# A gated recurrence with a fused two-layer product on one core: the engine queues from a listed order, more transposes by DMA, and casts shared between two engines

## The chip, the cores and the metric

The kernel runs on one core of a Trainium2 chip. The core has a matrix engine (PE, with its weight loads shown as PEld), a vector engine (DVE), a scalar engine (ACT), GpSimd (POOL), and a sync engine (SP) which here issues nearly all DMAs. Each engine works through its own instruction queue in program order, and waits in it on semaphores of other engines. The metric is the device time of one launch in microseconds (us), lower is better; a time is the median over several runs.

## What is computed

```python
for t in range(S):                                # S = 768, for 4 batches x 8 heads, D = 48
    state = alpha[t][:, None] * state + outer(k[t], v[t])
    y[t] = q[t] @ state
x = y.transpose(0, 2, 1, 3).reshape(3072, 384)    # tokens x (heads * D)
h = x @ w_in                                      # 384 -> 2048
g = relu(h) ** 2
out = g @ w_out                                   # 2048 -> 384, fp32
```

All inputs and the output are fp32. The kernel works in bf16 with fp32 sums.

## The kernel before

**Tiling.** The 3072 tokens are 24 chunks of 128, six for each batch. The recurrence is done chunk by chunk, all 8 heads at once; the state between chunks is kept in a PSUM bank (`st`). Chunks 0 to 3 are done as two sets of two with other code (`add_set`); chunks 4 to 23 with `add_chunk`. Two chunks share one scores step from chunk 8 on.

**One chunk** (`s`), in the words that the text below uses; the lines are those of the profile:

- Four loads of 192 KB (at, q, k, v; L388, in six buffers each), issued by SP.
- ln of alpha on ACT (L447), `p0`: its running sum on PE, exp of it and of its negative on ACT (`Af` L728, `Ainv` L735), v to bf16 on POOL (`vb` L716), and two tiny DMAs on POOL's queue for the row that decays the state (`ae` L746).
- q times `Af` and k times `Ainv` on DVE into `qk_s` (`mq` L777, `mk` L782).
- The transposes of both into `qkT`. For chunks 4 to 15: eight PE transposes (`p1q`, `p1k`, L298) and a DVE copy out of PSUM (`cp`, L714). For chunks 16 to 23: one transposing DMA on SP's queue, called a turn here (L799).
- `p2`: the scores on PE, then the causal mask. For chunks 4 to 7 both halves are DVE multiplies (L833); from chunk 8 the second half is an ACT copy (L836) and a select on POOL (L839).
- `ps`, the state's update: PE, DVE multiply (L867), ACT copy `sb` (L873). `p3a` and `p3b`: y on PE.
- y to bf16 (`xn`, L712, ACT), three PE transposes (`p4`, L298) and a copy of x transposed into `xT_big` (L714; DVE or ACT).

**The two products.** The tokens are taken in 12 groups: g0 holds chunks 0 to 3, g1 chunk 4, g2 chunk 5, g3 to g11 two chunks each. The first product (`add_moe1`, "M1") multiplies `w_in` with `xT_big` in blocks of 128 of the 2048 columns (f0 to f15); ACT does the relu (L990), DVE squares it into `gT` (L1009). The second product of g0 to g2 ("M2") is plain; from g3 on (`add_moe2_pair`) two chunks go together with seven block products P1 to P7 in place of eight, which need sums on DVE (S1 to S4, L1172 and L1182), four sums of `w_out` blocks done once (`foldT`, L1106), and small copies out of PSUM (ca, cu, cy, L1212/L1214, on ACT or DVE; c12, L1231/L1233; c11, c21 and c22, L1229, on DVE).

**The weights.** `w_in` comes in five pieces and `w_out` in four (L363), through four staging buffers; each piece is cast to bf16 by POOL (L366). The first two pieces of `w_in` hold two blocks each, the others four.

**What sets the order.** The kernel builds a list of operations (`Op`), each with an engine (or two to choose from), a planned duration, dependencies and buffers. `Plan.run` simulates the engines with these numbers and picks at each step, for the engine that comes free first, the operation that can start first (ties by a priority). It adds a slack of 0.25 to 0.3 us to waits of PE on other engines. The operations are then sorted by planned start and emitted, so that each engine's queue has this order. Loads keep the order in which they were added. Where the plan sees PE idle before the first M2, the program fills the idle time with dummy matmuls on a `warm` tile.

Of the kernel before, what the change touches and what calls it, by code (L numbers as in the profile page):

```python
# [64 lines left out]
class Plan:  # L65


    def __init__(self):
        self.pending = {}
        self.order = []  # L70
        self.free = {}
        self.pool = []
        self.outs = []
        self.wide = []

    def add(self, op):
        op.durs = op.eng if isinstance(op.eng, dict) else {op.eng: op.dur}
        for e in op.durs:
            self.pending.setdefault(e, []).append(op)
        return op  # L80
# [30 lines left out]
    def run(self, gate):  # L111
        free = self.free
        while any(self.pending.values()):
            best = None
            for eng, ops in self.pending.items():
                t0 = free.get(eng, 0.0)
                pick = None
                fifo = eng in ("DMA",)
                for op in (ops[:1] if fifo else ops):
                    if not gate(op):  # L120
                        continue
                    r = self.ready(op)
                    if r is None:
                        continue
                    if len(op.durs) > 1:
                        ends = {e: max(r, free.get(e, 0.0)) + x + LAT[e] for e, x in op.durs.items()}
                        if ends[eng] > min(ends.values()):
                            continue
                    key = (max(r, t0), op.prio)
                    if pick is None or key < pick[0]:  # L130
                        pick = (key, op)
                if pick is not None and (best is None or pick[0][0] < best[0]):
                    best = (pick[0][0], eng, pick[1])
            assert best is not None, "nothing can run"
            t, eng, op = best
            for e in op.durs:
                self.pending[e].remove(op)
            op.eng, op.dur = eng, op.durs[eng]
            while eng == "DMA" and self.outs and min(self.outs)[0] <= t:
                out = min(self.outs)  # L140
                self.outs.remove(out)
                t += out[1]
            op.start = t + getattr(op, "late", 0.0)
            if eng == "POOL":
                if not op.quiet:
                    self.pool.append((t, t + op.dur))
            elif eng == "DVE" and op.shared:
                for a, z in self.pool[-3:]:
                    op.dur += POOL_SHARE * max(0.0, min(z, t + op.dur) - max(a, t))
            free[eng] = t + op.dur  # L150
            if op.lat is None:
                op.lat = LAT.get(eng, 0.2)
            if eng == "OUT":
                self.outs.append((op.start, op.moves or op.dur))
            elif op.moves:
                self.outs.append((op.start + op.dur, op.moves))
            op.done = t + op.dur + op.lat
            if op.takes is not None:
                self.ready(op)
                for i, sl in enumerate(op.slots):  # L160
                    gives = op.gives if op.gives is not None else op
                    sl.release.append(gives[i] if op.n_slots > 1 else gives)
            self.order.append(op)
            self.on_pick(op)
        self.order.sort(key=lambda o: o.start)


@with_exitstack
def kernel(
# [33 lines left out]
    LB = 6  # L203
# [68 lines left out]
    CP_FLEX = 0  # L272
# [34 lines left out]
    SEL_FROM, SEL_T, SEL_N = 8, 0.6, 1  # L307
# [3 lines left out]
    VB_ACT = 99  # L311
# [4 lines left out]
    plan.slack = 0.3  # L316
    QT_FROM, QT_DMA, QT_LAT = 16, 1.8, 2.7
    XT_FROM, XT_DMA, XT_LAT = 99, 0.7, 2.3
# [16 lines left out]
    LD1 = 1.1  # L335
    LD2 = 1.5
    WLD = {"i": 2.05, "o": 2.4}
# [8 lines left out]
    SB = 4  # L346

    def load_w(which):
        j = len(w_ready[which])
        lo, hi = W_CUT[which][j:j + 2]  # L350
        n = hi - lo
        box = {}

        if which == "i":
            src, dst = w_in_r[:, :, lo * P:hi * P], w_in_b[:, :, lo * P:hi * P]
            shape = [P, KT, n * P]
        else:
            src, dst = w_out_r[:, lo:hi, :], w_out_b[:, lo:hi, :]
            shape = [P, n, d_model]

        def e_issue():
            box["w"] = stage.tile(shape, FP32, name=f"w{which}{n}", tag="stage")
            pin(nc.sync.dma_start(out=box["w"], in_=src))  # L363

        def e_cast():
            pin(nc.gpsimd.tensor_copy(dst, box["w"]))  # L366
        prev = w_cast[-SB] if len(w_cast) >= SB else None
        ld = add("DMA", WLD[which] * (0.85 if n < 4 else n / 4.0), e_issue, prev, lat=2.2)
        op = add("POOL", 0.1 + 0.32 * n, e_cast, ld, prio=-3.0)
        w_cast.append(op)  # L370
        w_ready[which].append(op)

    def w_dep(which, f):
        return w_ready[which][[hi > f for hi in W_CUT[which][1:]].index(True)]

    C = [dict() for _ in range(NT)]
    state = {}
# [3 lines left out]
    def add_load(s, nm):  # L381
# [8 lines left out]
        d["ld_" + nm] = add("DMA", LD if s < 4 else LD1, ld, prev, lat=L_ADD + (2.6 if s < 6 else 3.2 if s < 8 else 4.0), at=0.6)  # L390

    def add_decay2(s):
# [11 lines left out]
        ld = add("DMA", LD2, ld, C[s - LB]["use_at"] if s >= LB else None, lat=L_ADD + (2.6 if s < 6 else 3.2 if s < 8 else 4.0), at=0.6)  # L404
# [65 lines left out]
    def add_load2(u, nm, a=None):  # L470
# [8 lines left out]
        op = add("DMA", LD2 * (hi - lo) / H, ld, lat=2.5, at=0.6)  # L479
# [3 lines left out]
    def add_set(u):  # L483
# [163 lines left out]
        def add_out(c):  # L647
# [45 lines left out]
            p4.gives = xT  # L693
        for c in range(2):
            add_state(c)
            add_out(c)
        C[s0]["end"] = C[s0 + 1]["end"]
        for e in C[s0:s0 + 2]:
            e["use_at"], e["use_qt"], e["use_kt"], e["use_vt"] = ln[1], mq[1], mk[1], vb

    def add_chunk(s):
# [20 lines left out]
        vb = d["use_vt"] = add({"ACT": 0.37} if s >= VB_ACT else {"POOL": 0.5}, 0, e_vb, d["ld_vt"], *old, prio=-5.0)  # L722
# [60 lines left out]
        mq = d["use_qt"] = add("DVE", 0.767 if AMODE == "str" else 0.47, e_qA, a_, d["ld_qt"], *old_of(s, "p1q"), **g)  # L783
# [16 lines left out]
        if s < QT_FROM:  # L800
# [7 lines left out]
        if s >= QT_FROM:  # L808
# [7 lines left out]
        if s < QT_FROM:  # L816
# [6 lines left out]
        d["cps"] = [cp, cpk]  # L823
        yield
# [16 lines left out]
        done = after(p2, -0.15) if first else p2  # L841
        if s >= SEL_FROM and s % SEL_N == 0:
# [3 lines left out]
            p2.gives += [sm0, sc1]  # L846
        else:
            sm0 = add("DVE", 0.6, lambda: e_sm(0), done, **g)
            sm1 = add("DVE", 0.6, lambda: e_sm(1), done, after(sm0), **g)
            p2.gives += [sm0, sm1]  # L850

        if not last:
# [10 lines left out]
            ps = plan.add(Op("PE", 0.17, e_ps, [mk, vb, prev], lat=0.16, **g))  # L863
# [27 lines left out]
        if c > 0:  # L891
            p3a = plan.add(Op("PE", 0.17, e_p3a, [cp, C[s - 1]["sb"], after(sm0)], takes=GLA_BANKS, **g))
# [7 lines left out]
        xn = add("ACT", 0.36, e_xn, p3b, **g)  # L900
        (p3a or p3b).gives = xn

# [6 lines left out]
        if s >= XT_FROM:  # L909
            d["x"] = d["end"] = add("OUT", TURN, e_xturn, after(xn, 0.35), lat=XT_LAT)  # L910
            d["x"].moves = XT_DMA
            return
        p4 = plan.add(Op("PE", 0.165, e_p4, [xn], takes=GLA_BANKS, lat=0.14, **g))

        def e_xT():
            cast(xT, xT_big[:, :, xcols(s)], d["px"])
        xT = add({"ACT": 0.36, "DVE": 0.27} if s < XT_FLEX else {"DVE": 0.27}, 0, e_xT, p4, prio=-9.0)
# [3 lines left out]
    def add_scores(ss):  # L921
# [8 lines left out]
        p2 = Op("PE", 0.15 + 0.20 * len(ss), e_p2, [o for s in ss for o in C[s]["cps"]], takes=SC_BANKS, lat=0.10, prio=-10.0 + ss[0] * 0.01)  # L930
# [17 lines left out]
    OUT_LATE = 3.5  # L948
# [6 lines left out]
    sq = {}  # L955
    squares = []
# [5 lines left out]
    def add_moe1(g, f0, before, lo=0, hi=None, per=1):  # L962
# [5 lines left out]
        for i in range(per):  # L968
# [6 lines left out]
            deps = [C[s]["x"] for s in range(GT[g] + lo, GT[g] + hi)] + [w_dep("i", f0 + i)]  # L975
            deps += [after(op)] if op else []
            takes = M1_BANKS if i == 0 else None
            op = plan.add(Op("PE", 3 * n / 2400.0 + 0.01, e_mm, deps, takes=takes, prio=0.0, lat=0.10 if w < 512 else RL_LAT))
            op.moe = (1, (hi - lo) * 2.56 / FT)
            if i == 0:  # L980
# [11 lines left out]
        rl = add("ACT", 0.055 + w / 1190.0, e_relu, op, *old, *[after(x) for x in rs], prio=RELU_PRIO if g > 1 else RELU_PRIO0)  # L992
# [33 lines left out]
    def add_moe2(g, tt, before, box, quarters, pools):  # L1026

        for qd in quarters:
# [7 lines left out]
            deps = [o for f in fs for o in sq_of(g, tt, f)] + [w_dep("o", fs[-1] if g == 0 else FT - 1)] + ([after(before)] if before else [])  # L1036
# [4 lines left out]
            op.lat = 0.05  # L1041
# [20 lines left out]
        add("OUT", 0.65, e_out, ev, at=0.0).late = OUT_LATE if g > 2 else OUT_LATE1 if g else OUT_LATE0  # L1062
# [87 lines left out]
    def add_moe2_pair(tiles, before, T, pools):  # L1150
# [107 lines left out]
        for t, ready in ((0, (c11, c12)), (1, (c21, c22))):  # L1258
            def e_out(t=t):
                store(GT[tiles[t][0]] + tiles[t][1], box["ob", t])  # L1260
            add("OUT", 0.65, e_out, *ready, at=0.0).late = OUT_LATE
# [9 lines left out]
    P_PRIO = 0.0  # L1271
# [5 lines left out]
    FOLD_AT = 43  # L1277
# [45 lines left out]
    LEAD = 6  # L1323
# [14 lines left out]
    plan.run(gate)  # L1338
# [49 lines left out]
```

## Time and profile before

| | us |
|---|---|
| median of 3 runs | 179.13 |
| lowest and highest | 179.06, 180.19 |
| the profiled execution's own time | 179.53 |
| its span, first to last instruction | 177.8 |

| engine | busy us | share |
|---|---|---|
| PE | 169.2 | 95% |
| DVE | 147.8 | 83% |
| ACT | 127.9 | 72% |
| POOL | 57.9 | 33% |

The profile is of one execution; its span is 1.73 us shorter than its time. Matmuls are pipelined, so that a busy PE may still be waiting a little between two of them: the distance from the start of one matmul to the start of the next tells more than the busy time. SP's instructions are not counted as busy. In rows of groups, the numbers behind the bar are busy time and the mean duration in ns, then the idle time before and what ended it.

### The profile page before, as it was taken

The page shows a single profiled execution, that of the slowest core. Times are in us where ns is not written, and L with a number is a line of the kernel's source. Part 1 is how long each engine was busy: PE and PEld are TensorE (multiplying, and loading weights), DVE is VectorE, ACT ScalarE, POOL GpSimd, SP SyncE. Part 2 cuts the span into 40 slices and gives each one's busy share as a digit, 9 for nine tenths or more (in the row PEclk, how much of TensorE's full clock was granted, in tenths as well). Part 3 has the DMA queues.
Part 4 walks back from the last instruction along what each step waited for, and adds up shares of the span by engine and source line. Part 5 has one row for each costly group of instructions (what it writes and reads, how often), then busy time and mean ns, then how long its engine had stood idle before and what let it go on. Part 6 is the DMA issues. An engine that isn't in the chain of part 4 may idle for free.

```text
span 177.8 us, 5408 instructions
## 1 busy us (share of the span) xinstructions
PE 169.2 (95%) x2132; PEld 144.4 (81%) x2132; DVE 147.8 (83%) x264; ACT 127.9 (72%) x286; POOL 57.9 (33%) x97
## 2 busy tenths in 40 slices
PE   7898899999979999999999999999999999999992
PEld 2566688666767788889998898998999999999991
DVE  6599769748899999999989999999995999833920
ACT  4577469805867789996869896979987877647230
POOL 7011687181061146182218411430530610400100
PEclk9999999999999999999999999999999999999998
DMA  5999999999999998969999489989899846230504
GB/s 129 273 261 330 376 342 245 266 263 214 156 200 163 201 181 181 195 151 204 192 204 226 95 180 203 175 159 232 140 190 168 207 66 146 48 105 14 137 0 179
DMA packets 106937, 32.88 MB, mean 185 GB/s; under 512 B 99616, under 2 KB 105504, under 8 KB 106912
## 3 DMA queue, kind: packets, MB, share of 16 engines
q1 hardware_dynamic: 105600, 31.99, 84.7%
q0 software_dynamic: 1312, 0.55, 2.1%
q8 instruction: 16, 0.26, 0.7%
q14 instruction: 9, 0.07, 0.1%
HBM read 25.17 MB, written 4.72 MB: 168 GB/s over the span
## 4 chain that ended last, share of the span: by engine, by line
PE 76%; DVE 6%; SPq 5%; DMA 4%; ACT 3%; issue 2%; POOL 1%; POOLq 0%; DVEq 0%; ACTq 0%
PE bank L295 71%; SPq L478 5%; DMA wi<-in_moe_w_in_dram 4%; PE bank L298 4%; DVE qk_s L777 2%; DVE qk_s L782 2%; PE st L295 1%; DVE sm L833 1%; ACT r L990 1%; POOL sm L839 1%; ACT Af L728 1%; ACT L_s L447 1%; ACT sm L836 1%; POOL w_in_b L366 0%; DVE gT L1009 0%
## 5 line engine op out<-in xcount | busy, mean ns | idle before, releaser
L295 PE MATMUL bank<-xT_big,w_in_b 128*128 128x256 bf16 (+1 forms) x624 | 73.1, 264 | 0.7 <-POOL w_in_b L366 0.6
L990 ACT ACTIVATE r<-bank 128x512 bf16<-128x512 f32 x96 | 57.7, 620 | 12.9 <-PE bank L295 8.4
L295 PEld LDWEIGHTS <-w_in_b 128*128 128x128 bf16 x624 | 55.4, 98 | 7.6 <-POOL w_in_b L366 0.8
L1009 DVE TENSOR_TENSOR gT<-r 128x1024 bf16<-128x1024 bf16 (+1 forms) x49 | 38.1, 790 | 8.6 <-ACT r L990 8.6
L295 PEld LDWEIGHTS <-gT 128*128 128x128 bf16 x456 | 38.4, 98 | 5.1 <-issue 0.3
L295 PE MATMUL bank<-w_out_b,gT 128*128 128x192 bf16 (+1 forms) x312 | 40.1, 271 | 0.0
L746 POOL DMA_DIRECT2D ae_s<-Af x32 | 16.3, 512 | 35.4 <-ACT Af L728 35.4
L839 POOL TENSOR_SCALAR_AFFINE_SELECT sm<-sm 128x512 bf16<-128x512 bf16 x16 | 10.2, 658 | 35.9 <-ACT sm L836 35.9
L777 DVE TENSOR_TENSOR qk_s<-qt_s,Af 128x384 bf16<-128x384 f32 x20 | 18.3, 914 | 0.7 <-ACT Af L728 0.6
L833 DVE TENSOR_TENSOR sm<-bank,utri_b 128x512 bf16<-128x512 f32 x24 | 15.3, 681 | 1.8 <-PE bank L295 1.8
L716 POOL CAST vb<-vt_s 128x384 bf16<-128x384 f32 x20 | 12.6, 636 | 9.1 <-DMA vt_s<-in_v_dram 5.7
L295 PE MATMUL bank<-foldT,gT 128*128 128x192 bf16 x144 | 14.8, 246 | 0.0
L295 PE MATMUL bank<-foldT,sums 128*128 128x192 bf16 x144 | 14.5, 246 | 0.0
L712 ACT CAST xn<-bank 128x384 bf16<-128x384 f32 x20 | 10.1, 513 | 6.0 <-PE bank L295 6.0
L298 PE MATMUL bank<-ident_bf,qk_s 128*128 128x128 bf16 x128 | 11.8, 220 | 2.1 <-DVE qk_s L777 0.7
L782 DVE TENSOR_TENSOR qk_s<-kt_s,Ainv 128x384 bf16<-128x384 f32 x20 | 13.1, 657 | 0.0
L836 ACT CAST sm<-bank 128x512 bf16<-128x512 f32 x16 | 8.8, 614 | 5.0 <-PE bank L295 5.0
L295 PEld LDWEIGHTS <-sums 128*128 128x128 bf16 x144 | 12.0, 98 | 0.4
L298 PEld LDWEIGHTS <-qk_s 128*128 128x128 bf16 x128 | 8.2, 98 | 4.8 <-DVE qk_s L535 1.6
L728 ACT ACTIVATE Af<-bank 128x384 f32<-128x384 f32 x20 | 10.2, 508 | 1.5 <-PE bank L295 1.3
L295 PEld LDWEIGHTS <-qkT 64*128 64x128 bf16 (+1 forms) x228 | 8.8, 95 | 2.4 <-issue 1.4
L295 PE MATMUL bank<-vb,sm 128*128 128x48 bf16 (+1 forms) x224 | 10.0, 183 | 0.4 <-POOL sm L839 0.3
(96 smaller groups left out, 236.2 us busy)
## 6 DMA issues: line engine op xcount, KB each, us to landing
qt_s<-in_q_dram SPq DMA_DIRECT2D x22, 192.0 KB, 4.3
kt_s<-in_k_dram SPq DMA_DIRECT2D x22, 192.0 KB, 4.5
vt_s<-in_v_dram SPq DMA_DIRECT2D x20, 192.0 KB, 4.4
at_s<-in_alpha_dram SPq DMA_DIRECT2D x18, 192.0 KB, 4.1
out_dram<-ob SPq DMA_DIRECT2D x18, 192.0 KB, 2.3
wo<-in_moe_w_out_dram SPq DMA_DIRECT2D x4, 768.0 KB, 6.5
wi<-in_moe_w_in_dram SPq DMA_DIRECT2D x3, 768.0 KB, 8.1
at_s<-in_alpha_dram SPq DMA_DIRECT2D x3, 384.0 KB, 6.1
```

The costliest lines, as they stand in the source:

```text
L295: pin(nc.tensor.matmul(*a, **kw))
L298: pin(nc.tensor.transpose(*a))
L716: pin(nc.gpsimd.tensor_copy(out_t, in_t))
L728: pin(nc.scalar.activation(d["A"], a_in.rearrange("q (p j d) -> q j d p", p=NP, j=2), AF.Exp))
L746: pin(nc.gpsimd.dma_start(out=ae[64 * h:64 * h + D, h, :], in_=src))
L777: pin(nc.vector.tensor_mul(qA[:, :, 0:D].rearrange("q (p j) d -> q p j d", j=2), d["qt"].rearrange("q (p j) d -> q p j d", j=2), d["A"].re ...
L782: pin(nc.vector.tensor_mul(kI[:, :, 0:D], d["kt"], d["Ai"]))
L833: pin(nc.vector.tensor_mul(sm_half(hh), d["sc"][hh], utri_b.to_broadcast([P, NP, P])))
L836: pin(nc.scalar.copy(sm_half(1), d["sc"][1]))
L839: pin(nc.gpsimd.affine_select(out=sm_half(1), in_=sm_half(1), compare_op=ALU.is_ge, fill=0.0, base=0, pattern=[[0, NP], [1, P]], channel_m ...
L990: pin(nc.scalar.activation(R["r"][:, i0:i0 + w], box["ph"][:, 0:w], AF.Relu))
L1009: pin(nc.vector.tensor_mul(dst, r, r))
```

## The change

**The order.** `Plan.follow` takes the place of `Plan.run`. It walks a table `ORDER` of 1198 numbers, one for each operation in the order in which operations were added; `ENGINES` (124 digits) says for each operation with two possible engines which one it takes, and `PICKS` (263 digits) which PSUM bank each taker gets. It computes planned starts from the same kind of durations, without slack, and the emission is sorted by them as before. Dependencies for reused buffers (`ring`) are added to the plan, and a number of planned durations are changed.

```diff
+    def follow(self, order, engs, slots):
...
+        for op in self.all:
+            op.eng = list(op.durs)[int(next(engs)) if len(op.durs) > 1 else 0]
+            op.dur = op.durs[op.eng]
...
+        for i in order:
+            op = self.all[i]
+            eng = op.eng
+            t = max(op.at, free.get(eng, 0.0))
+            for d, x in op.deps:
+                t = max(t, d.done if x is None else d.start + d.dur + x)
...
+ORDER = [int(x) for x in """
+    0 1 2 3 4 8 5 9 10 11 13 25 14 15 16 17 20 12 23 26 21 22 6 18
...
-    plan.run(gate)
+    if ORDER:
+        plan.follow(ORDER, iter(ENGINES), iter(PICKS))
```

Read through the order of the `add` calls, the table gives each engine's queue. On PE, around chunks 6 to 9 and at the end:

```
... p1q 6, p1k 6, p4 5, M1 g1 f12 to f14, p1q 7, p1k 7, M1 g1 f15, M1 g2 f0, p2 of 6, M1 g2 f1 f2, p2 of 7 ...
... M1 g3 f0 to f5, ps 7, M1 g3 f6 f7, p1q 8, p1k 8, p1q 9, p0 10, p1k 9, M1 g3 f8 to f12, ps 8, p2 of 8 and 9 ...
... p4 23, P7 g9, P6 g9, M1 g11 f0 f1, P5 g9, P2 g10, M1 g11 f2 to f7, P3 g9, P4 g9, M1 g11 f8 to f15, then 13 products of g10 and g11
```

On DVE, from the k multiply of chunk 5 to the squares of g2 (`ev`: the copy of an output tile out of PSUM, which ACT did, L1056):

```
mk 5, cp 5, xT 4, ev g0 t0, ev g0 t1, stm 4, sm0 5, sm1 5, mk 6, mq 6, mq 7, mk 7, cp 6, cp 7, sm0 6, sm0 7, square g1, stm 6, square g1, fold T3 T2 T4, xT 6, square g2, square g2
```

The loads keep their order among themselves. The turns of chunks 14 and 15 stand among the loads of chunk 16; those of 16 and 17 before the q load of chunk 20; those of 18 and 19 before the k load of 21; those of 20 and 21 before the k load of 23. In the kernel before, the turn of a chunk stands among the loads of the second or third chunk behind it.

**Which engine does what.** Of operations that have a choice of two engines, DVE now takes three output copies (`ev`, g0 twice and g2), eight of the 27 small copies ca, cu and cy (one before), three of nine c12 (one before) and `xn` of chunk 4; of the copies of transposed x it has seven outside the sets (eight before) and ACT has nine (twelve before). The cast `vb` may go to ACT from chunk 4 on, and does so for chunks 5, 7, 11, 13, 16 and 22.

**Transposes and masks.**

```diff
-    SEL_FROM, SEL_T, SEL_N = 8, 0.6, 1
+    SEL_FROM, SEL_T, SEL_N = 6, 0.6, 1
-    QT_FROM, QT_DMA, QT_LAT = 16, 1.8, 2.7
-    XT_FROM, XT_DMA, XT_LAT = 99, 0.7, 2.3
+    QT = range(14, 40)
+    XT = (16, 18, 20, 22)
```

q and k of chunks 14 and 15 are transposed by DMA as well, and x of chunks 16, 18, 20 and 22 by a transposing DMA from `xn` into `xT_big` (no `p4`, no copy). The masks of chunks 6 and 7 are done as those of chunk 8.

**Casts of w_in and the last stores.** Of the first two pieces of `w_in`, POOL casts two thirds and ACT the last third.

```diff
+    CAST2 = (0, 1)
+        cut = KT - 1 if which == "i" and j in CAST2 else KT if which == "i" else n
+            pin(nc.gpsimd.tensor_copy(dst[:, 0:cut], box["w"][:, 0:cut]))
+            pin(nc.scalar.copy(dst[:, cut:], box["w"][:, cut:]))
```

The two output tiles of g11 are stored as four halves of 96 KB, each as soon as its copy is done, in place of two tiles of 192 KB.

## The prediction

> **What bounds the kernel now.** I read the page's table of engines first, then the chain of work that ended last, then the stretches of time, and then the rows of DVE and SP.
>
> ```profile
> PE 169.2 (95%) x2132; PEld 144.4 (81%) x2132; DVE 147.8 (83%) x264; ACT 127.9 (72%) x286; POOL 57.9 (33%) x97
> PE 76%; DVE 6%; SPq 5%; DMA 4%; ACT 3%; issue 2%; POOL 1%; POOLq 0%; DVEq 0%; ACTq 0%
> ```
>
> PE is the bound over the span. The shares hide three stages:
>
> ```profile
> 20.00:44.00 24.00, 23.94 (x242) 17.95 (x242) 16.58 (x21) 14.57 (x28) 13.24 (x11) 1.00 1.11 277
> 44.00:56.00 12.00, 11.11 (x177) 8.87 (x176) 11.32 (x17) 8.73 (x19) 3.45 (x6) 1.00 1.18 181
> ...
> 44.00:156.00 112.00, 110.35 (x1453) 97.80 (x1452) 107.14 (x181) 93.45 (x213) 37.36 (x65) 1.00 0.92 171
> ```
>
> The columns are length, then busy time of PE, PEld, DVE, ACT and POOL, clock, DMA share, GB/s. From 44 to 156 us DVE is busy 107.1 of 112: PE and DVE bound that stage together, and the DMA engines are full (1.18) in its first part. Before 20 us the loads lead, and behind 156 PE is alone.
>
> Distances from matmul start to matmul start show where PE waits. Against the median distance of each kind of matmul, the whole of it behind 22.99 us is 6.67 us too long. Waits over 0.15 us are 2.78 of that: 1.54 at 49.3 to 52.5 (PE waits for q and k multiplies), 0.49 at 78.3 (mask on POOL), 0.58 at 97.2 (q multiply), 0.17 at 113. The chain shows the same places:
>
> ```profile
> 46.25 0.93 DVE sm L833 x2
> ...
> 47.44 0.68 DVE gT L1009
> 48.12 0.20 DVE foldT L1106
> ...
> 48.91 0.17 DVE qk_s L777
> ```
>
> The first DVE stall has masks, a square and a fold ahead of the multiplies of chunk 6.
>
> **The change, part by part.** The sum is made against the profiled execution (179.53 us, span 177.8); it lies 0.40 us above the median, which I take off at the end.
>
> *Transposes that leave PE.* Chunks 14 and 15 lose 16 transposes, in the chain 0.22 us for four: 0.88. Four chunks lose three each, 0.17 for three: 0.67. PE has 1.55 us less to do, at a stage where it is 110.35 of 112 busy: -1.55. Left out as well are two DVE copies of 0.68 and four smaller ones.
>
> *What the transposes cost instead.*
>
> ```profile
> L799 SPq EVENT_SEMAPHORE  x8: 672/1492/2932, 98.0 to 144.0; - x8
> L799 SPq DMA_TRANSPOSE qkT<-qk_s x8: 1232/1238/1347, 101.0 to 146.2; - x8
> ```
>
> Each turn holds SP's queue for 1.24 us and waits 0.67 to 2.93 us ahead of that; everything queued behind it on SP (loads of q, k, v and alpha, stores) waits too. With 3.2 us to landing against 0.22 + 0.22 + 0.68 us for the PE path, a turn is some 2 us later for p2. One moves 1088 packets and fills 16 DMA engines for 1.74 us (143.95 to 146.0, nothing else under way). For x, with 384 columns in place of 1024, I take 0.65 by size; the ends are 0 and 1.74. Six more issues are 7.4 us of SP, and 2 x 1.74 + 4 x 0.65 = 6.1 us of DMA time. Between 100 and 156 us the DMA share is 0.80, so 11 us are free; k of chunk 16 landed at 93.6 and was used at 97.7, so loads have a lead of 4 us. I cost it at nothing; the cover is that lead. If it is used up, each late pair of chunks stops PE directly.
>
> The Trainium skill (Advanced Engine Details and Errata, X-Bar Transpose) has transposing DMAs as fast as plain ones, at 350 to 400 GB/s. Here one runs at about 160 GB/s, near the plain loads' 192 KB in 1.06 us; by the page the six would be an estimated 2.5 us of DMA time in place of 6.1, which leaves the sum as it is.
>
> *DVE, ACT and POOL.* DVE loses two qkT copies and two masks (4 x 0.68 = 2.72) and one x copy (0.35). It gains seven ca/cu/cy copies (0.355), two c12 (0.36), three output copies and an xn (0.557 by the nearest row, the cast of 128x384 out of PSUM): 5.4. Net +2.4 us, about +1.6 of it ahead of 156. ACT gains two mask copies (0.61), six vb casts (0.51) and two small casts (about 0.39), and loses 13 copies: -1.5 net. POOL loses six vb casts. DVE multiplies take 0.85 us alone and up to 1.50 beside a POOL operation, so six casts fewer on POOL give DVE back 0 to 6 x 0.65 us, and the two new selects take 0 to 1.3. I take the middle, +2.0 and -0.65, about -1.3: DVE's load ahead of 156 is even. Two squares and two sums of g10 and one sum of g9, now ahead of the last chunk's x copy (155.9), are listed behind it: 2 x 0.68 + 3 x 0.74 = 3.6 us of DVE move into the stage where it idles. So DVE could carry a stage shorter by about 4 us, not more.
>
> The Trainium skill (Perfetto Trace Analysis, Optimizing Scalar/DVE Operations) warns that moving work between GpSimd and DVE may not help, as they share a read port. The stretched multiplies (0.85 to 1.50) agree. By the rule the masks of chunks 6 and 7 save nothing (my sum gives them no term of its own) and the casts moved off POOL are the real relief.
>
> *The order.* Fold operations (4 x 0.95) are listed behind the multiplies of chunks 6 and 7 and their masks; now three of them run at 42.8 to 49.0, ahead of those. Two output copies of 0.56 come in their place. In the listed order k of chunk 11 is transposed at about 66 us by the PE work listed ahead of it, now at 73.4; later chunks too are further ahead. So the 2.78 us of named waits should go; the 3.89 us of small ones I leave, since the listed order plans without slack and DVE stays full. Bounds: 0 (every wait comes back elsewhere) and -6.67. Taken: -2.78. What is late next is the loads: k of chunk 7 landed at 48.8, k of 11 at 65.9, just when the listed order wants them.
>
> *Start.*
>
> ```profile
> 17.80 0.83 POOL L366 CAST w_in_b<-wi 128x768 bf16<-128x768 f32 x1 [0.29 <-DMA wi<-in_moe_w_in_dram]
> ...
> 20.93 1.47 POOL L366 CAST w_in_b<-wi 128x1536 bf16<-128x1536 f32 x1 [1.21 <-DMA wi<-in_moe_w_in_dram]
> ...
> 22.33 0.60 PE L295 MATMUL bank<-warm 128*128 128x256 bf16 x4
> ```
>
> The two split casts end 0.28 us earlier (a third of 0.83), but the next piece lands at 20.88 and its cast, which is not split, ends at 22.40 in any case: hidden. PE now does four dummies and starts the block on that piece at 22.99. Without the dummies it would start at 22.46: -0.53; the ends are 0 (dummies stay) and -0.53, and I take the latter since the listed order has M1 directly behind.
>
> *End.* The last store is 96 KB: 2.2 us to landing by the row of 12 such stores, 2.3 for 192 KB: -0.10.
>
> Sum: 179.53 - 1.55 - 0.53 - 2.78 - 0.10 = 174.57, less 0.40 for the median: 174.2 us.
>
> **The rivals.**
>
> *Everything closes up.* All 6.67 us go: 174.2 - 3.9 = 170.3 us. For it: PE's stretches at 80 to 90 and 140 to 150 us show waits of only 0.04, so the floor is low. Against: DVE has 4.9 us idle in the 112.
>
> *DVE and the loads hold the pace.* PE's 1.55 us and half of the waits (1.4) come back as waits for DVE or for loads in the stretch with DMA share 1.18: 174.2 + 3.0 = 177.2 us, around the edge of 1%.
>
> *Turns ahead of the loads (slower).* A turn that waits for its k multiply holds the loads behind it on SP. If the 4 us of lead are gone from chunk 14 on, five pairs of chunks each stop PE for about 2 us, the median wait and issue of a turn (1.5 + 1.2, less what other work covers): 174.2 + 10 = 184 us. It decides from 1.0 us a pair (4.9 us over five). For it: 20.1 us of SP waits stand on turns already, and six turns are added. Against: the listed order has loads one or two chunks further ahead of the turn of a given chunk than now.
>
> The Trainium skill (VectorE: DVE Perf Modes, Rules for kernel authors) prefers TensorE for a 128x128 transpose when the result may go to PSUM; that speaks for this rival, and the 3.2 us to landing agree with it as to delay, not as to PE time.
>
> *New waits equal the gain*: a listed order without slack on a chip that strays from its planned durations; 6.67 waits grow by 4.9 to 11.6, and the time stays at about 179.
>
> **How the numbers follow.** Forecast (172 to 176.5): 0.50. All closes up: 0.08. Pace held at 177.2: 0.20, half of it on each side of 1%. No gain, 179: 0.06. Slower, 184: 0.16. About 1% is what a measurement of this kernel tells from no change. Faster by over 1%: 0.50 + 0.08 + 0.10 = 0.68; within 1%: 0.10 + 0.06 = 0.16; slower: 0.16. The range runs from 170.8 to 181, which leaves out little below and most of the slower case above. The forecast's own range is 172.0 to 176.5: from the named waits plus half of the small ones gone, to the named ones half back with the dummies kept.
>
> **What would show it.** Right: eight PE transposes fewer for each of chunks 14 and 15; matmul distances with under 4 us of waits behind the start of M1; no wait over 0.3 us at chunks 6 and 7; M1 running through from 22.5. Wrong: PE waiting for qkT or xT_big from a DMA, or ACT and DVE for loads, behind 90 us (turns); waits of PE on DVE spread over 44 to 156 with DVE without any idle time (pace); dummies still ahead of 22.99.

## The result and the profile after

The changed kernel takes **181.05 us** (median of 6 runs, 180.41 to 181.25), the kernel before 179.06 in the same measurement: a ratio of 1.0095, 95% interval 1.0067 to 1.0124. It is about 1% slower, where 174.2 us was forecast. Where some executions of a kernel ran at a lower granted clock, the times and ratios below leave them out. The profiled execution took 181.01 us with a span of 179.3, against 179.53 and 177.8.

The table of engines and the chain that ended last, after:

```profile
PE 169.0 (94%) x2105; PEld 142.3 (79%) x2105; DVE 150.2 (84%) x272; ACT 126.2 (70%) x280; POOL 59.0 (33%) x93
PE 75%; DMA 9%; DVE 8%; issue 3%; ACT 2%; DVEq 0%; ACTq 0%
```

PE has 27 instructions fewer (28 transposes less, one dummy more), and yet it is busy about as long, 169.0 us against 169.2: the profile counts a PE that waits inside a pipelined row as busy. DMA was 4% of the chain and is 9%. The stretches, with those of 60 to 100 and 130 to 160 us added (columns as before the change):

```profile
20.00:44.00 24.00, 24.00 (x244) 17.38 (x241) 17.61 (x25) 13.14 (x26) 12.00 (x10) 1.00 1.07 278
44.00:56.00 12.00, 12.00 (x193) 9.91 (x192) 11.10 (x18) 10.77 (x25) 4.57 (x7) 1.00 1.09 176
60.00:100.00 40.00, 38.30 (x493) 32.60 (x492) 39.39 (x63) 35.01 (x80) 14.88 (x23) 1.00 1.04 183
130.00:160.00 30.00, 28.69 (x375) 25.99 (x373) 23.73 (x42) 22.41 (x51) 8.30 (x14) 1.00 0.73 138
44.00:156.00 112.00, 108.99 (x1417) 95.72 (x1416) 104.31 (x178) 93.10 (x211) 39.18 (x61) 1.00 0.97 174
```

The kernel before has in the third and the fourth of them:

```profile
60.00:100.00 40.00, 39.25 (x505) 34.62 (x504) 38.99 (x66) 34.42 (x81) 16.02 (x28) 1.00 1.01 192
130.00:160.00 30.00, 30.00 (x383) 28.11 (x381) 24.61 (x46) 22.02 (x51) 7.50 (x12) 1.00 0.65 131
```

At 44 to 56 the order did what it was forecast to do: PE is busy all 12 us where it was busy 11.11. At 60 to 100 it lost about as much again: 38.30 of 40 where it was 39.25, with DVE at 39.39 and the DMA engines at 1.04. At 130 to 160 it lost 1.31 us more, and there DVE has over 6 us of idle time. PE's waits by releaser, after, from 22 us on (us in total, times, longest):

```profile
PE bank L407 <- DVE qk_s L914: 1.1, 2, 0.7
PE bank L404 <- DMA xT_big<-xn: 0.5, 1, 0.5
PE bank L404 <- DMA qkT<-qk_s: 0.4, 1, 0.4
PE bank L404 <- DVE ob L1378: 0.4, 1, 0.4
PE bank L404 <- ACT r L1136: 0.3, 1, 0.3
PE bank L407 <- ACT xn L844: 0.3, 1, 0.3
```

They lie at 67.7, 79.0, 89.0, 90.7, 130.3, 137.2 and 150.3 us; none of them was there before. Excess here means matmul start distances above the median of their kind (same tiles and same shape), behind the start of M1; grouped so, the kernel before has 6.3 us, where the prediction has 6.67. It went to 8.4 us: from 2.46 to 0.64 at 44 to 56, from 2.07 to 3.83 at 56 to 100 and from 0.47 to 2.47 at 130 to 160. The seven waits are 4.2 us of it: 2.4 for the four at 60 to 100, 0.55 for the one at 130.3, 1.3 for the two turns at 137.2 (x) and 150.3 (q and k).

The end grew as well. SP's queue, after (start, duration), and then before:

```profile
173.96 1.17 SPq L1412 DMA_DIRECT2D out_dram<-ob  x2
175.18 0.42 SPq L1166 DMA_DIRECT2D out_dram<-ob  x1
175.65 1.14 SPq L1170 DMA_DIRECT2D out_dram<-ob  x2
```
```profile
172.72 2.35 SPq L1020 DMA_DIRECT2D out_dram<-ob  x4
```

The last matmul ends at 174.24 (174.32 before), but behind the last half store (L1412) three more stores are issued: one of g10 (L1166) and the two halves of a tile of g0 (L1170), whose rows had been ready for over 100 us. From the last matmul's end to the end of the span it is 5.06 us in place of 3.50.

In the prediction's terms, on the profiled execution: start -0.44 (M1 runs through from 22.55), end +1.56, and from the start of M1 to the last matmul +0.35. The 28 transposes, at 0.055 us each, are -1.55 of this, as forecast, so the waits are +1.9 (the excess by kind gives +2.1). Together that is +1.5, the difference of the spans.

### The profile page after: what moved, and what is told of

The parts are those of the page before. It is cut to its first block, busy times and chain, and to the rows that moved or that the text cites. A ratio compares the mean times of both kernels' runs of the same rounds, so it can differ in the third digit from the quotient of the medians.

```text
span 179.3 us, 5313 instructions
## 1 busy us (share of the span) xinstructions
PE 169.0 (94%) x2105; PEld 142.3 (79%) x2105; DVE 150.2 (84%) x272; ACT 126.2 (70%) x280; POOL 59.0 (33%) x93
## 4 chain that ended last, share of the span: by engine, by line
PE 75%; DMA 9%; DVE 8%; issue 3%; ACT 2%; DVEq 0%; ACTq 0%
PE bank L404 68%; PE bank L407 5%; DMA qt_s<-in_q_dram 3%; DMA xT_big<-xn 3%; DMA qkT<-qk_s 2%; PE st L404 2%; DMA out_dram<-ob 1%; DVE sm L729 1%; DVE gT L1155 1%; DVE sm L967 1%; DVE qk_s L914 1%; ACT r L1136 1%; DVE qk_s L909 1%; DVE qk_s L657 1%; DVE st L1006 1%
## 5 line engine op out<-in xcount | busy, mean ns | idle before, releaser
L1136 ACT ACTIVATE r<-bank 128x512 bf16<-128x512 f32 x96 | 55.4, 612 | 10.1 <-PE bank L404 8.9
L1155 DVE TENSOR_TENSOR gT<-r 128x1024 bf16<-128x1024 bf16 (+1 forms) x49 | 36.8, 767 | 3.1 <-ACT r L1136 3.0
L973 POOL TENSOR_SCALAR_AFFINE_SELECT sm<-sm 128x512 bf16<-128x512 bf16 x18 | 13.6, 764 | 37.4 <-ACT sm L970 37.2
L909 DVE TENSOR_TENSOR qk_s<-qt_s,Af 128x384 bf16<-128x384 f32 x20 | 19.4, 981 | 2.7 <-ACT Af L860 2.4
L848 POOL CAST vb<-vt_s 128x384 bf16<-128x384 f32 x14 | 11.6, 842 | 12.9 <-DMA vt_s<-in_v_dram 12.9
L970 ACT CAST sm<-bank 128x512 bf16<-128x512 f32 x18 | 10.1, 594 | 1.8 <-PE bank L404 1.5
L407 PE MATMUL bank<-ident_bf,qk_s 128*128 128x128 bf16 x112 | 9.6, 220 | 1.8 <-DVE qk_s L914 1.1
L407 PEld LDWEIGHTS <-qk_s 128*128 128x128 bf16 x112 | 6.8, 98 | 4.2 <-DVE qk_s L914 1.7
L1006 DVE TENSOR_TENSOR st<-st,ae_s 128x384 f32<-128x384 f32 x16 | 9.0, 560 | 1.3 <-PE st L404 0.9
L867 ACT ACTIVATE Ainv<-bank 128x384 bf16<-128x384 f32 x20 | 10.0, 506 | 0.0
```

Source lines behind the costliest of these rows:

```text
L407: pin(nc.tensor.transpose(*a))
L848: pin(nc.gpsimd.tensor_copy(out_t, in_t))
L909: pin(nc.vector.tensor_mul(qA[:, :, 0:D].rearrange("q (p j) d -> q p j d", j=2), d["qt"].rearrange("q (p j) d -> q p j d", j=2), d["A"].re ...
L970: pin(nc.scalar.copy(sm_half(1), d["sc"][1]))
L973: pin(nc.gpsimd.affine_select(out=sm_half(1), in_=sm_half(1), compare_op=ALU.is_ge, fill=0.0, base=0, pattern=[[0, NP], [1, P]], channel_m ...
L1006: pin(nc.vector.tensor_mul(st4, st4, bcast(ae.rearrange("q j p -> q p j"), D)))
```

## The experiments

Ratios are to the kernel before on the same chip, with 95% intervals.

**Stores at the end.** `st.late` is added to a store's planned start when the operations are sorted; in a listed order it comes on top of a place that is late already.

```diff
-        st.late = OUT_LATE if g > 2 else OUT_LATE1 if g else OUT_LATE0
+        st.late = OUT_LATE if g > 2 else OUT_LATE1 if g else 0 if tt == 1 else OUT_LATE0
...
-                sts[t][0].late = OUT_LATE
+                sts[t][0].late = 0 if gl == NG - 2 else OUT_LATE
```

> The changed kernel with the planned delay taken off two stores only: the fourth output tile of g0 and the tiles of g10, so that they stand ahead of the last half tile in SP's queue and not behind it. Theory A (the end of the changed kernel is lengthened by three stores that are issued behind the last half tile; last matmul ends at 174.24 but the span at 179.30, a tail of 5.06 us against 3.50 before): the tail goes to 3.3 to 3.6 us and the time falls by 1.5 us, to 179.5. Rival (the tail is the transfer of the last halves itself): within 0.4 us of 181.05.

Measured: 179.04 us, ratio 1.0006 (0.9983 to 1.0029). The half stores are last on SP:

```profile
173.24 0.38 SPq L1166 DMA_DIRECT2D out_dram<-ob  x1
173.72 0.88 SPq L1412 DMA_DIRECT2D out_dram<-ob  x2
```

The tail is 3.14 us, 1.9 less. The time is 2.0 us under the 181.05, and 1.4 under it when the same kernel was run again (e1_again, below): so much were the stores. The excess of PE is still 7.8, so the rest has another cause. All later edits of the changed kernel but e2 start from this one.

**The parts without the listed order**, and two parts alone.

```diff
-    if ORDER:
+    if not ORDER:
```

> The changed kernel with all its parts, but with its queues ordered by the plan's own picking as in the kernel before, not by the listed order. Theory A (the parts save PE work, and the listed order loses it again to waits on DVE between 60 and 100 us and to late stores): about 178, below the kernel before by 0.5 to 1.5 us. Rival B (the parts themselves cost it: turns by DMA and more copies on DVE): 180 to 182, no better than the listed order.

182.57 us, 1.0179 (1.0145 to 1.0213), excess 9.3, and M1 starts 1.5 us later (24.04). The same parts take 3.5 us more in the simulated order than in the listed one of e1_stores. In the kernel before, `QT_FROM` 14 in place of 16, and x of four chunks turned, re-ordered by its own `Plan.run`:

> The kernel before with one part alone: q and k of chunks 14 and 15 by DMA as well. Theory A: PE loses 0.88 us of transposes and DVE 1.36 us of copies in a stage where both are full: 0.5 to 1.2 us faster than before, 178 to 178.6. Rival B (turns hold the loads behind them on SP, or come late for the scores): 0.3 to 2 us slower than before.

> The kernel before with one part alone: x of chunks 16, 18, 20 and 22 by DMA. Theory A: PE loses 0.67 us; the first product of these chunks waits for the landing (in the changed kernel one such wait of 0.68 us shows at 137.2), so within 0.7 us of before. Rival B (each turn of x stops PE by about that much): 1 to 3 us slower than before.

182.81, 1.0212 (1.0189 to 1.0234), and 180.33, 1.0067 (1.0043 to 1.0091). `Plan.run` moved other work too (waits for small ACT copies at the end), so these tell little of the turns. With the order of before kept and only the instructions replaced in place:

```diff
+        elif s in (14, 15):
+            cp = cpk = add({"DVE": 0.61}, 0, e_turn, p1k, **g)
+            p1q.emit = p1k.emit = lambda: None
```

> The kernel before in its own order, in which only q and k of chunks 14 and 15 are turned by DMA at the place where their copies out of PSUM stood; nothing else is moved (in the run e3_qk14 the plan re-ordered all that follows). Theory A (the turn is a gain of PE and DVE time and the loss of e3_qk14 came from the new order): 0.3 to 1.2 us faster than before. Rival B (the turn is late for the scores or holds the loads): 1 to 4 us slower than before, with PE waiting for qkT at about 94 to 104 us.

> The kernel before in its own order, in which only x of chunks 16, 18, 20 and 22 is turned by DMA at the place where its copy out of PSUM stood. Theory A (0.67 us of PE gained, no wait of M1, since the order has other products between): 0 to 0.7 us faster. Rival B (M1 waits for landings of 3 us): 1 to 4 us slower, PE waiting for xT_big four times.

181.96, 1.0173 (1.0119 to 1.0227; three runs), and 181.45, 1.0151 (1.0112 to 1.0191). PE's waits for turns in the two (the granted clock of the profiled execution was 0.988 in e5, 1.00 in e6):

```profile
PE bank L295 <- DMA qkT<-qk_s: 3.0, 2, 2.6
```
```profile
PE bank L295 <- DMA xT_big<-xn: 3.1, 2, 1.9
```

In place of a PE transpose and a copy, one turn makes PE wait 2.6 us in e5, and two of four do so for 1.9 and 1.2 us in e6. In the listed order the 14 turns together cost PE 0.9 us of idle time: it has other PE work in between.

**One resource relieved at a time, in the listed order.** First, 11 copies from DVE to ACT, each at its place:

```diff
+        for i in (146, 692, 695, 757, 801, 806, 851, 891, 897, 987, 1043):
+            plan.all[i].eng = "ACT"
```

> The run e1_stores with eleven copies moved from DVE's queue to ACT's at the same places (three output copies, xn of chunk 4, the seven small copies ca, cu, cy up to g8 and c12 of g3), so that DVE has some 4.9 us less to do, all but nothing else. Theory A (between 60 and 100 us DVE has no idle time and holds the pace, and the copies that the change gave it are what PE waits for): the waits of 67.9 and 79.1 us shrink and the time falls by 0.7 to 2 us below e1_stores, to 177 to 178.3. Rival (DVE is full of necessary work in the right order; ACT gets late instead): within 0.5 us of e1_stores, 179.

181.52, 1.0133 (1.0089 to 1.0177): slower than e1_stores, though on another chip (e5 to e8 share one on which e1_stores was not run). The waits for `qk_s` fell from 1.1 to 0.4, and others came:

```profile
PE bank L404 <- DMA xT_big<-xn: 1.0, 2, 0.7
PE bank L404 <- ACT cy L1361: 0.9, 1, 0.9
PE bank L404 <- ACT L_s L569: 0.6, 1, 0.6
```

Then x of the four chunks back on PE (three transposes and an ACT copy where the turn stood):

```diff
...
+            d["x"].emit = lambda: None
+            p4 = d["p4"] = Op("PE", 0.18, e_p4)
+            xT = d["xT"] = Op("ACT", 0.36, e_xT)
...
```

> The run e1_stores with x of chunks 16, 18, 20 and 22 turned on PE again (three transposes and an ACT copy each at the place of the DMA). Theory A (one wait of 0.46 us for xT_big goes, 0.67 us of PE work comes back): within 0.5 us of e1_stores. Rival B (the turns of x also delay loads and the turns of q and k behind them on SP, and with them PE at 150 us): 0.5 to 2 us faster than e1_stores.

181.29, 1.0147 (1.0101 to 1.0193). The waits for `xT_big` are gone, and yet the excess is 8.2 and the time no better: in this order the x turns are no loss. Then, in e11, the stores around the x turn moved on SP, and in e12 all added delays of stores taken away:

```diff
+        for j, k in enumerate((8, 9, 7, 6)):
+            obs[k][1][0].start = C[18]["x"].start + 0.02 * (j + 1)
+        C[20]["x"].start = C[22]["cp"].start + 0.02
+        plan.order.sort(key=lambda o: o.start)
```

> The kernel of e1_stores, in which on SP alone the four full stores planned around 126 to 128 are issued behind the x turn of chunk 18, and the x turn of chunk 20 is issued behind the qk turn of chunk 22; nothing else moves. Theory A: the waits of PE around 137 and 150 (0.5 and 0.4 us, together an excess of 1.40 over 130 to 160) come from the stores that share the DMA engines with the x turn while it is in flight, and from a qk turn that is queued behind the wait of an x turn; then the two go, and the time falls by 0.6 to 1.2 us: about 178.1. Rival B: the turns land as late in any place, since what holds them is their own 256-byte packets and the moment when xn and qk are written; then it is within 0.3 us of e1_again, or the waits come at the loads that are pushed back.

```diff
-            op.start += getattr(op, "late", 0.0)
+            op.start += 0.0
```

> The kernel after the change, in which no store is put behind the place that the list gives it (the 2 us and 32 us that are added to the listed place are gone for every store; e1_stores did this for g10 and one tile of g0 alone). Theory A: at the end it is as e1_stores, and the stores around 126 to 128 leave 2 us sooner and are out of the way of the x turn of chunk 18, so 0.2 to 0.8 us under e1_again. Rival B: a store at its listed place waits on SP for its rows and holds the loads and turns behind it; then it is 0.3 to 1.5 us over e1_again, with waits of PE for xT_big, qkT or a load.

186.04, 1.0402 (1.0360 to 1.0443), and 181.88, 1.0154 (1.0110 to 1.0199). Both theory As fell. For e12 the profile does not show why: its profiled execution was the fastest of the six, 180.17 us, with waits like those of e1_again. In e11, from 130 to 165:

```profile
PE bank L404 <- DMA xT_big<-xn: 2.1, 1, 2.1
PE bank L404 <- DVE ob L1378: 1.7, 2, 1.3
PE bank L404 <- DMA qkT<-qk_s: 0.6, 1, 0.6
```

The x turn of chunk 20, now behind a turn that itself waits, landed later. PE's waits from 22 us on sum to 6.3 us where e1_again has 3.0. The profiled execution is 8.1 us over that of e1_again, and its granted clock was lower as well (0.972; 0.86 up to 20 us). So 3.3 of the 8.1 us are waits, and how much of the rest is the clock was not separated.

**DVE beside POOL, and the loads.** A close look at one wait, after: DVE, POOL and PE around 79 us.

```profile
77.13 2.19 DVE L909 TENSOR_TENSOR qk_s<-qt_s,Af 128x384 bf16<-128x384 f32 x2
79.25 1.01 DVE L914 TENSOR_TENSOR qk_s<-kt_s,Ainv 128x384 bf16<-128x384 f32 x2
```
```profile
77.18 0.65 POOL L973 TENSOR_SCALAR_AFFINE_SELECT sm<-sm 128x512 bf16<-128x512 bf16 x1
```
```profile
79.85 0.40 PE L407 MATMUL bank<-ident_bf,qk_s 128*128 128x128 bf16 x4 [0.67 <-DVE qk_s L914]
```

PE waits 0.67 us for a product that stands behind two q products; they took 2.19 us where two take 1.7, and POOL's select ran beside the first. So the select was cut to one of four head pairs (the mask of the other three is left out), with every queue in its order:

```diff
-            pin(nc.gpsimd.affine_select(out=sm_half(1), in_=sm_half(1), compare_op=ALU.is_ge, fill=0.0,
-                                        base=0, pattern=[[0, NP], [1, P]], channel_multiplier=-1))
+            pin(nc.gpsimd.affine_select(out=sm_half(1)[:, 0:1], in_=sm_half(1)[:, 0:1], compare_op=ALU.is_ge, fill=0.0,
+                                        base=0, pattern=[[0, 1], [1, P]], channel_multiplier=-1))
```

> The kernel of e1_stores, in which POOL's select of the masked scores handles one of a half's four head pairs (the mask of the other three pairs is left out, so the output differs from the reference); every queue keeps its order, and DVE and ACT keep all their work. Theory A: the waits on DVE that took the place of those at chunks 6 and 7 are there because copies and products of DVE are stretched while POOL works beside them (1.29, 1.44 and 1.12 us in place of 0.55 to 0.85); a select falls from 0.65 to about 0.2 us, DVE loses most of its stretch beside selects, and the excess of 56 to 100 (2.01 us in e1_stores) falls by 0.7 to 1.5: about 177.7 us, 0.7% under e1_again. Rival B: the waits are those of the listed order itself, which has ACT, DVE and the loads close to PE at the same places, and POOL's select has no part in them: within 0.4 us of e1_again, with the waits at the same instructions.

> The kernel of e1_stores again, on the chip of the three others, as what they are compared with. All theories expect the time of the kernel before within 0.4 us (ratio 0.998 to 1.003), with the same waits of PE as in e1_stores (0.7 us twice for DVE qk_s between 65 and 80, 0.4 for a turn of q and k).

e9: 179.52, 1.0021 (0.9988 to 1.0054); e1_again: 179.66, 1.0039 (1.0014 to 1.0064). No difference. But the waits are not the same ones, against rival B's wording. e9, 60 to 100:

```profile
PE bank L404 <- DMA qkT<-qk_s: 1.6, 2, 1.0
PE bank L404 <- ACT L_s L569: 0.7, 1, 0.7
PE bank L407 <- DVE qk_s L914: 0.2, 1, 0.2
```

The waits for DVE shrank from 1.1 to 0.2; PE ran ahead into a late alpha load (ACT's `L_s` had waited 1.17 us for it) and into turns that took 5.5 us to land there in place of 3.6. So the loads were relieved, alone and together with the select, and the kernel before got the same cuts. From chunk 6 on a load brings 64 of its 128 rows, so half of the input is left out:

```diff
-            pin(nc.sync.dma_start(out=d[nm], in_=SRC[nm][b, c]))
+            pin(nc.sync.dma_start(out=d[nm][0:HP], in_=SRC[nm][b, c][0:HP]) if s >= LB else nc.sync.dma_start(out=d[nm], in_=SRC[nm][b, c]))
```

> The kernel of e1_stores, in which every load of q, k, v and alpha of one chunk from chunk 6 on moves 64 of the 128 rows (the other rows keep an earlier chunk's values, so the output differs from the reference); each queue keeps its order. Theory A: the DMA engines set the pace of 44 to 140 (their share of busy time is 1.00 to 1.05 in each stretch of it); turns and loads land late because they queue behind loads, and what is gained on DVE or POOL is lost there, as in e9. With half of the packets gone the share falls under 0.7, the waits for xT_big and qkT and most of the waits on ACT and DVE behind late loads go, and the excess behind 22.99 falls from 8.3 to under 6: 176.5 to 177.5 us. Rival B: the loads are not late; the waits are those of DVE and ACT in the listed order, and the time stays within 0.5 us of e1_stores (179.0 to 179.7), with the same two waits for qk_s at 67 and 79.

> The kernel of e9_less_sel (POOL's select on one of four head pairs) with the same cut of the loads (64 of 128 rows from chunk 6 on); both leave part of the work out. Theory A: in e9 the waits for DVE at 67 and 79 shrank or went, but waits for turns came in their place; with the DMA engines relieved as well nothing takes their place, and it is 1 to 2 us under e15: 175 to 176 us. Rival B: as e15 within 0.5 us, other waits of the listed order show up.

> The kernel before the change with the same cut of its loads (64 of 128 rows from chunk 6 on; the output differs from the reference). Theory A: it was held by the same DMA share (0.83 to 1.12 in 44 to 140), so it falls as well, but by less than e15, since it has 14 fewer transposing transfers in the same queue: 177.5 to 178.5 us, and e15 ends under it by about the 1.5 us of PE work that the change takes away. Rival B: unchanged within 0.5 us of before (179).

> The kernel before the change with both cuts of e17 (loads of 64 of 128 rows from chunk 6 on, POOL's select on one of four head pairs; parts of the work are left out, as there). Theory A: the order before the change is held by its own places (PE waits at 49 to 53 for multiplies that stand behind a fold, 1.5 us; none of the two cuts is there), so it falls by 0.3 to 1.2 us: 177.8 to 178.6, and e17 stays 1 to 2 us under it, which is what the change is worth where DVE and the transfers have room. Rival B: the two cuts help any order alike: it falls by about 2 us to 177, as e17, and the change is worth nothing even then.

> e17 again, on the chip of e18, for the comparison: 176.5 to 177.2 us by all theories.

| | select whole | select a quarter |
|---|---|---|
| listed order, whole loads | e1: 1.0006 (0.9983 to 1.0029), 1.0039 (1.0014 to 1.0064) | e9: 1.0021 (0.9988 to 1.0054) |
| listed order, half loads | e15: 1.0029 (1.0001 to 1.0058) | e17: **0.9891** (0.9862 to 0.9921), **0.9851** (0.9803 to 0.9899) |
| order of before, half loads | e16: 1.0036 (1.0013 to 1.0059) | e18: 0.9998 (0.9974 to 1.0023) |

In us: e15 179.26, e16 179.71, e17 176.84 and 176.65, e18 179.41. The stretch of 60 to 100 shows how; e1_again, e9, e15, e17, e18, in this order:

```profile
60.00:100.00 40.00, 38.28 (x494) 32.60 (x493) 39.38 (x64) 34.99 (x80) 14.86 (x24) 1.00 1.02 184
```
```profile
60.00:100.00 40.00, 37.41 (x483) 32.13 (x481) 36.25 (x64) 34.93 (x78) 14.38 (x23) 1.00 1.07 181
```
```profile
60.00:100.00 40.00, 38.69 (x499) 32.91 (x497) 39.41 (x64) 35.38 (x80) 16.39 (x25) 1.00 0.47 94
```
```profile
60.00:100.00 40.00, 39.93 (x528) 34.76 (x526) 38.29 (x68) 36.94 (x84) 16.92 (x28) 1.00 0.54 103
```
```profile
60.00:100.00 40.00, 39.41 (x510) 34.88 (x509) 38.36 (x66) 34.73 (x81) 14.56 (x28) 1.00 0.48 102
```

With the shorter select alone DVE, with the same 64 instructions, is busy 3.1 us less and has 3.75 us of idle time, but the DMA share is 1.07 and PE is busy even less. With half loads alone the DMA share is 0.47, but DVE is as full as before and PE still waits. With both, PE is busy 39.93 of 40, and the excess of 56 to 100 falls from 3.6 (e1_stores) and 3.8 (e1_again) to 1.6 (1.7 in e17_again), under the 2.1 of the kernel before. In this stretch the two are limits of about the same height. The select's cut frees POOL as well as DVE, and the two were not separated; no wait of PE for POOL shows there, though. In the order of before, PE's waits at 49 to 53 stay (2.5 us of excess at 44 to 56 in e16 and e18 as in before), so neither cut helps, and the fall that theory A had for e16 and e18 did not come.

The waits at 130 to 160 are another matter. The one for `ob` is gone in e9 and e17, so it hung on DVE. The one for the x turn at 137 has 1.1 us of excess in e1_again, 0.7 in e9, 0.5 in e15, 1.0 in e17 and none in e17_again; its cause stays open.

So e17_again stands under e18 by 1.5%, 2.8 us, on one chip: that is what transposes, order, start and end are worth where DVE and transfers have room. Little of it is the order. Of the 2.8 us between the profiled executions of e17 and e18, 0.8 lie ahead of M1, 1.6 are less PE work, 0.25 the tail and 0.1 the excess; in the profiled execution of e17_again, the fastest of its six, the excess is 1.5 less than in e18. No version that does the whole work and beats the kernel before was found.

## Why the prediction was wrong

*Transposes that leave PE (-1.55)*: held. PE has 16 and 12 transposes fewer.

*Turns, costed at nothing*: too low. Two of the seven waits after are for turns, 0.9 us of idle time and 1.3 us of excess; the lead of 4 us that was to cover them is one of the loads, and these waits are for the landing of the turns themselves. Without an order made for them they cost about 2.7 us (e5, e6). Of the 10 us of the rival with turns ahead of the loads little was seen.

*DVE, ACT and POOL, costed even*: the sum was on the safe side and its use wrong. Over 44 to 156 DVE's busy time fell (107.14 to 104.31). But the sum was made over 112 us, and four of the seven waits came in the 40 of them in which DVE had 0.6 us of idle time and the DMA engines were full.

*The order (-2.78)*: **the step that failed first.** The waits at chunks 6 and 7 went, as worked out. The prediction then left all other distances as they were; they grew, and the term measured +1.9. It had said itself that the order plans without slack and DVE stays full, and priced that at nothing. e17 shows that price for the stretch of 56 to 100: with the room given, 2.0 to 2.3 us of excess go there. Even then the term is far from -2.78: against e18 the excess is 0.1 us less in e17 and 1.5 in e17_again. Whether planned slack would have kept the waits away was not tested.

*Start (-0.53)*: -0.44.

*End (-0.10)*: **the second step that failed**, at +1.56. It asked how large the last store is and not which stores stand behind it. With the delay taken off (e1_stores) it is -0.36.

The rival in which new waits equal the gain came nearest to the time (179), in part by luck, since it had no late stores; without these the kernel takes 179.0 to 179.7. The one with DVE and the loads holding the pace named the cause for 60 to 100. They had chances of 0.06 and 0.20. No rival had the stores at the end.

## What to carry to other kernels

An order found against planned durations has to hold where engines slow each other down. Look for the stretch where a second engine has next to no idle time (here 0.6 us in 40), and price the new order there and not over the span. If a relief of one resource changes nothing, see whether the waits are still the same ones; if they moved, relieve two at once before calling the first one innocent. When a list fixes places, read what else is added to them before the emission is sorted, and look at which transfers are last in the queue.

## What the runs showed of the hardware

POOL work stretches some DVE instructions and not others. e1_again, durations in ns, shortest, median and longest:

```profile
L909 DVE TENSOR_TENSOR qk_s<-qt_s,Af x20: 837/866/1426, 33.5 to 145.3; 128x384 bf16<-128x384 f32 x20
```
```profile
L967 DVE TENSOR_TENSOR sm<-bank,utri_b x22: 675/682/692, 38.4 to 153.2; 128x512 bf16<-128x512 f32 x22
```

The product of two SBUF tiles goes from 0.84 to 1.43 us, and each one over 1.1 us ran beside a cast or a select of POOL; the mask, which reads one operand from PSUM, stays within 0.02, beside a select too. It works the other way as well: two casts of `vb` (about 0.5 us each alone) took 3.44 us while the q products beside them kept 0.87 and 0.88, after:

```profile
58.51 3.44 POOL L848 CAST vb<-vt_s 128x384 bf16<-128x384 f32 x2
```

The Trainium skill (GPSIMD Engine Reference, 1. Specifications) says that POOL contends with DVE instructions that have two SBUF inputs; these rows agree.

The DMA engines are full at quite different rates: share 1.07 at 278 GB/s in 20 to 44 (with the weights), 1.04 at 183 GB/s in 60 to 100 (q, k, v and alpha). A packet has 495 bytes on average in the first (6.68 MB in 13,506) and 214 in the second (7.32 MB in 34,227). The Trainium skill (DMA: Bandwidth & Descriptors, Specifications) puts full rate at 512 bytes and more; that the smaller packets go at the lower rate agrees.
